# Attention with memory and a feed-forward block: second buffers for the loads of k and v

## The chip, the cores and the metric

One core of a Trainium2 chip. The core has a matrix engine (TensorE, PE; PEld are its weight loads), a vector engine (VectorE, DVE), a scalar engine (ScalarE, ACT), a general engine (GpSimd, POOL) and a queue engine (SyncE, SP), which here issues every transfer between memory and the core's on-chip memory (SBUF). Each engine works through its own instructions in order and waits for the others by semaphores. Matrix products land in accumulator banks (PSUM). The metric is the time of one execution on the device in microseconds (us).

## The reference

The attention is computed for 4 batches and 8 heads of 576 tokens and 64 columns; its output is the input of a feed-forward block over 2304 tokens.

```python
scores = scale * np.matmul(q, k.transpose(0, 1, 3, 2))      # causal mask, softmax -> a
local = np.matmul(a, v)
mem_ret = np.einsum('bhsd,bhde->bhse', q_p, M_prev)          # q_p = phi(q), phi(x) = elu(x) + 1
mem_norm = np.einsum('bhsd,bhd->bhs', q_p, z_prev)[..., None] + 1e-06
x = g * mem_ret / mem_norm + (1 - g) * local                 # g = sigmoid(beta), one per head
h = x @ w_in                                                 # 512 -> 2048
out = np.maximum(h, 0.0) ** 2 @ w_out                        # 2048 -> 512
```

## The kernel before

The work has four kinds of pieces.

*The weights.* w_in and w_out arrive as 64-bit floats in 32 pieces of 512 KB (`load_weight`, L197: tiles raw, xw, hw) and each is split into a high and a low part by DVE and ACT (`split_weight`, L167 to L173, tile w). The pieces come in four stages; the raw tiles of a later stage lie where those of an earlier stage lay, so they can be loaded when these have been split. raw23 is the first piece of the third stage.

*The first tokens.* Tokens 0 to 63 of every head are done at the start in one go (`first_tokens`), in a pool `tp` of their own that is given back afterwards. mask0 is the causal mask of their 64 by 64 scores.

*The attention units.* 24 units, each of a batch, a pair of heads and two or four query tiles (tiles 1 and 2, or 3 and 4, of 128 tokens). `loads` brings a unit's k (kd, L340), its memory and q (qm, L344) and its v (vv, L347). In `attention` PE makes scores (sp, L468), DVE masks and reduces them (L472), ACT takes the exponential (L484); DVE finds the largest entry of v (vx, L400) and makes a scaled copy of v in 16 bits (vs, L417); the probabilities are split (L521, L523), transposed by a transfer (aT, L527) and multiplied with v on PE (acc, L548 to L553), summed on DVE (s, L555), and added by POOL to the memory's share (pm, L435; memx, L560). The result is stored to memory (xd, L572). The first two units use v itself (L542) instead of vs. The next unit's loads are asked for in the middle of a unit. q has two buffers, kd and vv one each.

*The feed-forward blocks.* Nine blocks of 256 tokens (`moe`): tiles of up products (L626 to L628), the square of the positive part on ACT, POOL and DVE, and down products (L616 to L618). Block 0 is the first tokens. The tokens of block 1 are those of units 0 to 3, and `prefetch` loads them back (xn, L592) and transposes them on PE (px, L595).

The order on each engine isn't the order of the code: a scheduler simulates the program at build time with its own costs and issues what it finds ready, by the place in the code as priority. A buffer that is free earlier moves instructions on all engines. On SP the transfers are issued strictly in that order, so one that waits for its buffer holds up all behind it.

Of the kernel before, what the change touches and what calls it, by code (L numbers as in the profile page):

```python
# [8 lines left out]
F32 = mybir.dt.float32  # L9
# [8 lines left out]
B, H, S, D = 4, 8, 576, 64  # L18
# [3 lines left out]
P = 128  # L22
# [21 lines left out]
PXE = 'aa'  # L44
PHI = 1
QB = 2
VVB = 1
ZW = D + 1
MW = 576
WSC = 1.0 / 256.0  # L50
EB = 3
RB = 1
KB = 1
XB = 2
PJ = 6
SEQ = 'a0 b0 g a1 r b1 r c0 l r r c1'
# [34 lines left out]
def fused_kernel(ctx: ExitStack, tc: tile.TileContext, t0_d, zt_d, kk_d, qv_d, beta, w_in, w_out, out):  # L91
    nc = tc.nc
    w_in = w_in.bitcast(U32)
    w_out = w_out.bitcast(U32)
    cp = ctx.enter_context(tc.tile_pool(name="cp", bufs=1))
# [11 lines left out]
    mask = cp.tile([P, MW], BF16, name="mask")  # L107
# [19 lines left out]
    def gates():  # L127
# [9 lines left out]
        for b in range(GB):  # L137
            nc.vector.tensor_copy(gpb[:, b * NP : (b + 1) * NP], gp)
        nc.vector.tensor_scalar(out=g1b, in0=gpb, scalar1=-1.0, scalar2=1.0, op0=ALU.mult, op1=ALU.add)

    mask0 = cp.tile([P, D], F32, name="mask0")
    nc.vector.tensor_copy(mask0[:D], mask[:D, 448 : 448 + D])
    nc.vector.tensor_copy(mask0[D:], mask[D:, 512 : 512 + D])

    wsrc = []
    for j in range(4):
# [52 lines left out]
    def weights():  # L199
        n0 = 0  # L200
        for n, ex in STG:
            n1 = n0 + n + len(ex)
            dpl = ctx.enter_context(tc.tile_pool(name=f"wd{n0}", bufs=1, reuse_waits="tile"))
            plain = range(n0 + len(ex), n1) if XF else range(n0, n0 + n)
            heads = []
            for m in range(n0, n1):
                if m in wt:
                    continue
                two = PAIR and m % 2 == 0 and m in plain and m + 1 in plain and m >= PAIR - 1
                wp[m] = dpl.tile([P, 2, 1024 if two else 512], F32R, name=f"w{m}")  # L210
                heads.append(m)
                for u in range(2 if two else 1):
                    wt[m + u] = wp[m][:, :, u * 512 : (u + 1) * 512]
            with ExitStack() as st:
                tp = st.enter_context(tc.tile_pool(name="tp", bufs=1, reuse_waits="tile")) if n0 == 0 else None
                spl = st.enter_context(tc.tile_pool(name=f"ws{n0}", bufs=1, reuse_waits="tile")) if n else None
                where = list(ex) + [spl] * n if XF else [spl] * n + list(ex)
                if n0 == 0:
                    first_tokens(tp, lambda: load_weight(heads[len(raw)], where[heads[len(raw)]]))
                    yield  # L220
                for m in range(n0, n1):
                    if m in heads:
                        if m not in raw:
                            load_weight(m, where[m - n0])
                        split_weight(m)
                    yield
            n0 = n1

    def first_tokens(tp, ahead):
        me, ze, se, xe, ye = ([nc.gpsimd if c == "p" else nc.vector for c in t] for t in TE)  # L230
        xh = mo.tile([P, NK, BLK], F32R, tag="xh", name="xh", bufs=2)
        xl = mo.tile([P, NK, BLK], F32R, tag="xl", name="xl", bufs=2)
        xq.append((xh, xl))
        ng = B // GB
        bc = [P, GN, D]
        tr, sp, wt0, wx = ({} for _ in range(4))
# [100 lines left out]
    def loads(b, p, tiles):  # L337
        qa, qb = QT[tiles[0]][0], sum(QT[tiles[-1]])
        kd = at.tile([P, S], F32, tag="kd", name="kd", bufs=KB)
        nc.sync.dma_start(kd[:, :qb], kk_d[b, p, :, :qb])  # L340
        qm = at.tile([P, 2 * ZW + SQ], F32, tag="qm", name="qm", bufs=QB)
        qa, qb = qa - D + 2 * ZW, qb - D + 2 * ZW
        for c0, c1 in [(0, qb)] if qa == 2 * ZW else [(0, 2 * ZW), (qa, qb)]:
            nc.sync.dma_start(qm[:, c0:c1], qv_d[b, p, :, c0:c1])  # L344
        vv = at.tile([P, 5 * P], F32, tag="vv", name="vv", bufs=VVB)
        nv = (tiles[-1] + 1) * P
# [431 lines left out]
```

## Time and profile before

| | |
|---|---|
| median of three runs | 617.59 us (617.44 to 619.06) |
| the profiled execution | 617.12 us, of which the span from first to last instruction is 615.0 us |
| PE busy | 567.4 us (92%) |
| DVE busy | 403.6 us (66%) |
| ACT busy | 329.8 us (54%) |
| POOL busy | 186.9 us (30%) |
| mean granted clock of PE | 0.980 of full speed |

An engine's busy time is read against a stretch and not against the whole: the kernel's start is work of DVE and ACT, its end is work of PE alone. The matmuls overlap in the array, so busy time says where PE idles, not how fast it goes; the granted clock says that.

### The profile page before, as it was taken

The page shows a single profiled execution, that of the slowest core. Times are in us where ns is not written, and L with a number is a line of the kernel's source. Part 1 is how long each engine was busy: PE and PEld are TensorE (multiplying, and loading weights), DVE is VectorE, ACT ScalarE, POOL GpSimd, SP SyncE. Part 2 cuts the span into 40 slices and gives each one's busy share as a digit, 9 for nine tenths or more (in the row PEclk, how much of TensorE's full clock was granted, in tenths as well). Part 3 has the DMA queues.
Part 4 walks back from the last instruction along what each step waited for, and adds up shares of the span by engine and source line. Part 5 has one row for each costly group of instructions (what it writes and reads, how often), then busy time and mean ns, then how long its engine had stood idle before and what let it go on. Part 6 is the DMA issues. An engine that isn't in the chain of part 4 may idle for free.

```text
span 615.0 us, 11584 instructions
## 1 busy us (share of the span) xinstructions
PE 567.4 (92%) x4198; PEld 482.9 (79%) x4198; DVE 403.6 (66%) x1247; ACT 329.8 (54%) x748; POOL 186.9 (30%) x179
## 2 busy tenths in 40 slices
PE   2267899599999998999999999999999999999997
PEld 2156797388888886888888888788888899998996
DVE  3999878677779876988788787797887511001000
ACT  1597777465676744666566544665466412322312
POOL 1410305226563651224331323232322121221221
PEclk9996799899999999999999999999999999999999
DMA  5939296577556755577555555665546320200000
GB/s 179 400 145 377 49 269 147 130 139 163 122 116 145 174 100 130 125 162 150 134 114 131 100 129 122 142 181 122 112 89 117 74 48 1 68 1 1 35 0 35
DMA packets 128392, 76.54 MB, mean 124 GB/s; under 512 B 99920, under 2 KB 113232, under 8 KB 128336
## 3 DMA queue, kind: packets, MB, share of 16 engines
q1 hardware_dynamic: 128336, 75.81, 49.9%
q8 instruction: 33, 0.54, 0.4%
q14 instruction: 23, 0.19, 0.1%
HBM read 42.76 MB, written 8.91 MB: 84 GB/s over the span
## 4 chain that ended last, share of the span: by engine, by line
PE 78%; DMA 8%; DVE 8%; issue 2%; POOL 1%; ACT 1%; SPq 1%; DVEq 0%; POOLq 0%; ACTq 0%
PE up L626 11%; PE up L628 11%; PE up L627 11%; PE oacc L616 10%; PE oacc L618 10%; PE oacc L617 10%; PE sp L468 7%; DMA vv<-in_qv_dram 3%; PE acc L553 2%; PE pm L435 2%; DMA aT<-a 2%; DMA raw<-in_w_in_dram 2%; PE acc L550 1%; PE acc L548 1%; PE acc L542 1%
## 5 line engine op out<-in xcount | busy, mean ns | idle before, releaser
L626 PE MATMUL up<-xh,w 128*128 128x256 f32 x576 | 166.9, 290 | 0.7 <-DVE xl L599 0.6
L628 PE MATMUL up<-xh,w 128*128 128x256 f32 x576 | 166.1, 288 | 0.0
L627 PE MATMUL up<-xl,w 128*128 128x256 f32 x576 | 165.6, 288 | 0.0
L641 POOL TENSOR_TENSOR gl<-r,gh 128x512 fp32r<-128x512 f32 x72 | 100.1, 1390 | 207.2 <-DVE gh L640 121.4
L626 PEld LDWEIGHTS up<-xh,w 128*128 128x128 f32 x576 | 110.8, 192 | 8.6 <-issue 4.3
L484 ACT ACTIVATE e<-e,mx 128x320 f32<-128x320 f32 (+3 forms) x128 | 77.9, 611 | 71.8 <-DVE mx L472 70.6
L616 PE MATMUL oacc<-w,gh 128*128 128x512 f32 x288 | 115.4, 401 | 0.4 <-ACT gh L638 0.4
L627 PEld LDWEIGHTS up<-xl,w 128*128 128x128 f32 x576 | 110.8, 192 | 4.8 <-issue 2.0
L628 PEld LDWEIGHTS up<-xh,w 128*128 128x128 f32 x576 | 110.8, 192 | 3.9 <-issue 2.9
L617 PE MATMUL oacc<-w,gh 128*128 128x512 f32 x288 | 113.8, 395 | 0.0
L618 PE MATMUL oacc<-w,gl 128*128 128x512 f32 x288 | 110.2, 397 | 0.3 <-POOL gl L641 0.3
L632 ACT ACTIVATE r<-up 128x512 f32<-128x512 f32 x72 | 42.6, 592 | 112.1 <-PE up L628 104.1
L523 DVE SCALAR_TENSOR_TENSOR a<-e,a 128x128 f16<-128x128 f32 x120 | 78.7, 669 | 25.4 <-ACT a L521 25.1
L634 POOL TENSOR_TENSOR r<-r 128x512 f32<-128x512 f32 x40 | 45.0, 1124 | 136.5 <-ACT r L632 136.5
L640 DVE CAST gh<-r 128x512 fp32r<-128x512 f32 x40 | 16.9, 423 | 93.8 <-ACT r L636 90.6
L616 PEld LDWEIGHTS oacc<-w,gh 128*128 128x128 f32 x288 | 54.3, 189 | 11.5 <-issue 1.5
L618 PEld LDWEIGHTS oacc<-w,gl 128*128 128x128 f32 x288 | 53.0, 188 | 12.6 <-issue 1.4
L617 PEld LDWEIGHTS oacc<-w,gh 128*128 128x128 f32 x288 | 54.3, 189 | 9.2 <-issue 0.7
L472 DVE CUSTOM_DVE_ANT_0 e<-sp,mask 128x320 f32<-128x320 f32 (+3 forms) x128 | 56.6, 474 | 7.3 <-PE sp L468 6.9
L521 ACT ACTIVATE a<-e 128x128 f16<-128x128 f32 x120 | 57.0, 522 | 3.2 <-DMA aT<-a 1.7
L553 PE MATMUL acc<-vs,aT 128*128 128x128 f16 x308 | 37.0, 221 | 0.0
L550 PE MATMUL acc<-vs,aT 128*128 128x64 f16 x308 | 35.7, 193 | 0.0
(130 smaller groups left out, 883.0 us busy)
## 6 DMA issues: line engine op xcount, KB each, us to landing
raw<-in_w_in_dram SPq DMA_DIRECT2D x11, 512.0 KB, 8.7
vv<-in_qv_dram SPq DMA_DIRECT2D x16, 320.0 KB, 2.9
raw<-in_w_out_dram SPq DMA_DIRECT2D x9, 512.0 KB, 7.0
kd<-in_kk_dram SPq DMA_DIRECT2D x16, 288.0 KB, 3.1
xd<-memx SPq DMA_DIRECT2D x32, 128.0 KB, 2.1
xn<-xd SPq DMA_DIRECT2D x16, 256.0 KB, 3.0
out_dram<-o SPq DMA_DIRECT2D x16, 256.0 KB, 2.2
qm<-in_qv_dram SPq DMA_DIRECT2D x8, 321.0 KB, 3.2
```

Of the source, the lines that this page charges most:

```text
L472: nc.vector.tensor_tensor_reduce(out=e[:n, h, ks], in0=sps[:n, h, :w], in1=mask[:n, 448 - q0 + s * w : 448 - q0 + s * w + w], scale=-0.125 ...
L484: nc.scalar.activation(e[:n, h, :ke], e[:n, h, :ke], AF.Exp, bias=bs, scale=-1.0, accum_out=sm[:n, h : h + 1])
L521: nc.scalar.mul(av[:, :, o0 : o0 + w], x, SC)
L523: nc.vector.scalar_tensor_tensor(out=av[:, :, o0 + w : o0 + 2 * w], in0=x, scalar=SC, in1=av[:, :, o0 : o0 + w], op0=ALU.mult, op1=ALU.sub ...
L553: nc.tensor.matmul(o2, aT[:, h * nb + c, :n], vs[:, h, c], start=False, stop=c == i)
L616: nc.tensor.matmul(acc[t], gh[:, u, ts], w_out_op(f, 0), start=f == 0, stop=False)
L617: nc.tensor.matmul(acc[t], gh[:, u, ts], w_out_op(f, 1), start=False, stop=False)
L618: nc.tensor.matmul(acc[t], gl[:, u, ts], w_out_op(f, 0), start=False, stop=f == NF - 1)
L626: nc.tensor.matmul(up[:, u, :], w_in_op(f, k, 0), xh[:, k, :], start=k == 0, stop=False)
L627: nc.tensor.matmul(up[:, u, :], w_in_op(f, k, 0), xl[:, k, :], start=False, stop=False)
L628: nc.tensor.matmul(up[:, u, :], w_in_op(f, k, 1), xh[:, k, :], start=False, stop=k == NK - 1)
L641: nc.gpsimd.tensor_tensor(out=gl, in0=r, in1=gh.bitcast(F32), op=ALU.subtract)
```

## The change

kd and vv get a second buffer each, and mask0 moves from the pool that lives as long as the kernel into the first tokens' pool, made there by the same two copies. Lines after it move up by four and, behind first_tokens, by one.

```diff
-VVB = 1
+VVB = 2
-KB = 1
+KB = 2
...
-    mask0 = cp.tile([P, D], F32, name="mask0")
-    nc.vector.tensor_copy(mask0[:D], mask[:D, 448 : 448 + D])
-    nc.vector.tensor_copy(mask0[D:], mask[D:, 512 : 512 + D])
...
+        mask0 = tp.tile([P, D], F32, name="mask0")
+        nc.vector.tensor_copy(mask0[:D], mask[:D, 448 : 448 + D])
+        nc.vector.tensor_copy(mask0[D:], mask[D:, 512 : 512 + D])
```

The order of the instructions that come out of the scheduler moves at many places. On SP, in the first 20 us, behind the first tokens' last load; kd_327, qm_329 and vv_331 are the loads of unit 1. Before:

```order
L258 DMA tr1_120<-in_t0_dram 128x1024
L344 DMA qm_329<-in_qv_dram 128x386
L197 DMA raw4_363<-in_w_out_dram 128x1024
L197 DMA raw5_379<-in_w_out_dram 128x1024
L197 DMA raw6_408<-in_w_out_dram 128x1024
L197 DMA raw7_415<-in_w_out_dram 128x1024
L197 DMA raw8_430<-in_w_in_dram 128x1024
L197 DMA xw_463<-in_w_in_dram 128x512
L197 DMA xw_464<-in_w_in_dram 128x512
L340 DMA kd_327<-in_kk_dram 128x320
```

and with the change:

```order
L257 DMA tr1_120<-in_t0_dram 128x1024
L339 DMA kd_327<-in_kk_dram 128x320
L343 DMA qm_329<-in_qv_dram 128x386
L346 DMA vv_331<-in_qv_dram 128x384
L193 DMA raw4_363<-in_w_out_dram 128x1024
L193 DMA raw5_379<-in_w_out_dram 128x1024
L193 DMA raw6_408<-in_w_out_dram 128x1024
L193 DMA raw7_415<-in_w_out_dram 128x1024
```

kd_327 and vv_331 have moved ahead of the weights raw4 to raw8; vv_331 stood 23 rows further down, as the first row of the next piece.

On SP again, from there to the third stage's first weights, raw23; the numbers 776, 774 and 778 belong to unit 3, 481 to unit 2 and 870 and 872 to unit 4. Before:

```order
L347 DMA vv_331<-in_qv_dram 128x384
L344 DMA qm_776<-in_qv_dram 128x386
L572 DMA xd0_92<-memx_314 128x2x128
L340 DMA kd_774<-in_kk_dram 128x320
L347 DMA vv_481<-in_qv_dram 128x384
L527 DMA_TRANSPOSE aT_791<-a_790 128x10x128
L197 DMA raw23_663<-in_w_out_dram 128x1024
L197 DMA raw24_670<-in_w_in_dram 128x1024
```

and with the change:

```order
L343 DMA qm_776<-in_qv_dram 128x386
L571 DMA xd0_89<-memx_314 128x2x128
L339 DMA kd_870<-in_kk_dram 128x576
L346 DMA vv_778<-in_qv_dram 128x384
L526 DMA_TRANSPOSE aT_791<-a_790 128x10x128
L571 DMA xd0_89<-memx_448 128x2x128
L526 DMA_TRANSPOSE aT_791<-a_790 128x6x128
L343 DMA qm_872<-in_qv_dram 128x130
L343 DMA qm_872<-in_qv_dram 128x256
L193 DMA raw23_663<-in_w_out_dram 128x1024
L193 DMA raw24_670<-in_w_in_dram 128x1024
```

The loads of k and v are now those of one unit later, and unit 4's q (qm_872), which stood behind the third stage's weights, stands ahead of raw23.

On DVE, around unit 3's two last sums (s3_907 and s3_935), with unit 4's scores (e_1394) beside them. Before:

```order
L417 SCALAR_TENSOR_TENSOR vs_858<-vv_778,vy_848,vs_858 128x3x64 x2
L532 RECIPROCAL sm_879<-sm_879 128x2
L532 RECIPROCAL sm_913<-sm_913 128x2
L400 TENSOR_REDUCE vx_1326<-vv_875 128x1
L472 ISA e_1394,mx_1395<-sp_1397,mask_76 128x288
L472 ISA mx_1395 128x1
L402 TENSOR_SCALAR vx_1326<-vx_1326 128x1
L555 TENSOR_REDUCE s3_907<-acc_896 128x128
L555 TENSOR_REDUCE s3_935<-acc_928 128x128
```

and with the change:

```order
L471 ISA e_1394,mx_1395<-sp_1397,mask_76 128x288
L471 ISA mx_1395 128x1
L165 SCALAR_TENSOR_TENSOR xw_734<-xw_734 128x256
L163 TENSOR_SCALAR hw_726<-hw_726 128x512
L554 TENSOR_REDUCE s3_907<-acc_896 128x128
L554 TENSOR_REDUCE s3_935<-acc_928 128x128
L169 TENSOR_TENSOR w29_716<-hw_719,w29_716 128x512
L399 TENSOR_REDUCE vx_1446<-vv_1354 128x1
L389 SCALAR_TENSOR_TENSOR pe_1442<-qm_1351,pe_1442 128x256
L169 TENSOR_TENSOR w31_718<-xw_733,w31_718 128x256
L165 SCALAR_TENSOR_TENSOR hw_726<-hw_726 128x512
```

The reduction of the next unit's v no longer stands in front of the sums, and the last weight splits (L169, before L173) have moved behind them.

## Rows read from the trace of the kernel before

**Rows 1.** Windows: stretch, length, busy PE, PEld, DVE, ACT, POOL, clock, DMA, GB/s

```profile
0.00:46.10 46.10, 17.54 (x178) 12.92 (x178) 35.12 (x94) 25.97 (x57) 12.80 (x17) 1.00 0.65 241
57.70:124.20 66.50, 57.73 (x351) 46.81 (x349) 51.54 (x156) 45.38 (x105) 17.86 (x18) 0.91 0.61 164
124.20:230.00 105.80, 105.14 (x817) 88.51 (x816) 83.93 (x260) 67.26 (x164) 53.77 (x63) 0.99 0.64 136
230.00:247.00 17.00, 14.64 (x119) 12.11 (x118) 12.23 (x36) 8.40 (x19) 3.54 (x4) 1.00 0.55 134
247.00:615.00 368.00, 363.89 (x2709) 316.20 (x2707) 210.31 (x672) 174.25 (x382) 98.09 (x77) 1.00 0.41 91
...
15.40:30.80 15.40, 3.34 (x19) 1.75 (x16) 15.09 (x37) 9.05 (x18) 7.68 (x7) 1.00 1.03 400
```

**Rows 2.** Timeline of PE: start, length, instruction [idle before, what ended it]

```profile
63.21 2.52 PE L542 MATMUL acc<-vv,aF 64*128 64x64 f32 x12 [1.88 <-DMA vv<-in_qv_dram]
...
83.52 0.67 PE L435 MATMUL pm<-qm,pe 128*128 128x130 f32 x4
...
122.40 1.87 PE L468 MATMUL sp<-kd,qm 64*128 64x448 f32 x4 [4.96 <-DMA kd<-in_kk_dram]
124.20 1.26 PE L595 MATMUL px<-identr,xn 128*128 128x128 f32 x8
```

**Rows 3.** Windows behind those two idle times, columns as in rows 1

```profile
64.00:72.00 8.00, 8.00 (x40) 7.15 (x38) 8.00 (x20) 7.17 (x21) 2.83 (x2) 0.57 0.00 0
119.00:126.00 7.00, 3.60 (x23) 2.34 (x24) 3.48 (x13) 3.08 (x8) 0.00 (x0) 0.51 0.75 212
```

**Rows 4.** Timeline of SP's queue: issue, length, transfer

```profile
61.38 0.34 SPq L340 DMA_DIRECT2D kd<-in_kk_dram  x1
73.17 0.33 SPq L347 DMA_DIRECT2D vv<-in_qv_dram  x1
...
75.56 0.49 SPq L197 DMA_DIRECT2D raw<-in_w_out_dram  x1
...
84.22 0.81 SPq L344 DMA_DIRECT2D qm<-in_qv_dram  x2
...
118.21 0.38 SPq L572 DMA_DIRECT2D xd<-memx  x1
...
120.08 0.80 SPq L592 DMA_DIRECT2D xn<-xd  x2
```

**Rows 5.** Timeline of DVE: its waits on v and on the third stage's weights

```profile
76.51 0.55 DVE L400 TENSOR_REDUCE vx<-vv 128x1 f32<-128x384 f32 x1 [1.93 <-DMA vv<-in_qv_dram]
...
79.56 0.43 DVE L167 TENSOR_SCALAR raw<-raw 128x512 uint32<-128x512 uint32 x1 [1.07 <-DMA raw<-in_w_out_dram]
...
81.54 0.43 DVE L167 TENSOR_SCALAR raw<-raw 128x512 uint32<-128x512 uint32 x1 [1.50 <-DMA raw<-in_w_in_dram]
...
114.37 0.82 DVE L400 TENSOR_REDUCE vx<-vv 128x1 f32<-128x640 f32 x1 [2.94 <-DMA vv<-in_qv_dram]
...
115.92 0.75 DVE L555 TENSOR_REDUCE s<-acc 128x128 f32<-128x256 f32 x2
...
235.59 0.82 DVE L400 TENSOR_REDUCE vx<-vv 128x1 f32<-128x640 f32 x1 [2.76 <-DMA vv<-in_qv_dram]
```

**Rows 6.** Groups by line on DVE: shapes, count | busy us, mean ns | idle before

```profile
L405 DVE TENSOR_REDUCE vy<-vt 128x1 f32<-128x128 f32 x22 | 6.2, 281 | 1.9 <-PE vt L404 1.9
L169 DVE SCALAR_TENSOR_TENSOR hw<-hw 128x512 uint32<-128x512 uint32 x8 | 6.0, 745 | 0.0
L173 DVE TENSOR_TENSOR w<-hw,w 128x512 fp32r<-128x512 f32 x8 | 5.4, 680 | 0.0
L173 DVE TENSOR_TENSOR w<-xw,w 128x256 fp32r<-128x256 f32 x8 | 3.5, 442 | 1.2 <-ACT w L172 1.2
L402 DVE TENSOR_SCALAR vx<-vx 128x1 uint32<-128x1 uint32 x22 | 3.2, 145 | 0.1
L142 DVE CAST mask<-mask 64x64 f32<-64x64 bf16 x1 | 0.2, 186 | 0.0
```

## The prediction

> **What bounds the kernel now.** I read first the busy time of each engine by stretch, then the idle times of the matrix engine (TensorE, PE) in its timeline with what ended each, and last the queue of the loads (SP) and the vector engine (DVE) around those places.
>
> By stretch [rows 1]: up to 46.1 us PE works 17.5 us and DVE 35.1: the weights are split and the first tokens computed, and DVE is the limit (15.09 of 15.40 us between 15.4 and 30.8). From 57.7 to 124.2 PE works 57.73 of 66.50 us, 8.77 idle, at a mean clock of 0.91. After that it idles 0.66 of 105.8 us, 2.36 of the 17 us from 230 to 247, and 4.11 of the last 368, most of it the drain at the end. So from about 124 us on the kernel is as long as its matmuls; a change of buffers can win only what stands idle or runs slowly before 124 us, and the 2.4 us at 230 to 247.
>
> PE's idle times in the first place have names [rows 2]: 1.88 us until unit 1's v lands (63.21), and 4.96 us until a load of k lands (122.40), with the transposes of the next MoE block's tokens (px, 124.20) behind it. After each of the two the granted clock falls to 0.5, the lower level of 1.2 GHz [rows 3]: first between 64 and 72 us (the mean over 64 to 72 is 0.57, so (1 - 0.57) x 8 = 3.4 us of full-rate work is lost), and again from 119 (0.51 over 119 to 126).
>
> The cause is one step back, in SP's queue [rows 4]. With one buffer the load of unit 2's v waits for the last product with unit 1's v: SP stands from 61.38+0.34 to 73.17 and nothing behind it leaves, the first weights of the third stage (raw, 75.56) among them. DVE feels each such load [rows 5]: its reduction of v (vx) waits 1.93 us at 76.51, 2.94 at 114.37 and 2.76 at 235.59.
>
> **The change part by part.** *Where the mask lies.* The two casts (the first 186 ns, the second alike [rows 6]) stay at their place as the vector engine's second and third row and are read only by the first tokens' softmax: cost nothing. They free 256 bytes a partition for good, against 2304 + 2560 taken by the second kd and vv. No instruction is added; all the rest is order.
>
> *Unit 1's k and v* (160 + 192 KB) now stand before the four loads of w_out (raw4 to raw7), v having stood 23 rows further down the queue. So the 1.88 us wait on v goes. If the clock then stays up, 3.4 us more go: PE would be up to 5.3 us earlier by about 71 us. This is no gain of the total yet; what PE does next must be ready. What it may cost is the four weight loads behind: 352 KB at the 400 GB/s of 15.4 to 30.8 us is 0.9 us each. I take nothing, since DVE, which splits them, is busy 15.09 of 15.40 us there with work already landed; if that cover is gone, 0.9.
>
> The Trainium skill speaks against this part: "DMA: Bandwidth & Descriptors", section "Issuing engines are not separate DMA queues", says that all loads share the same 16 engines and interleave, so an earlier load is paid for by another. The trace agrees that they are full there (share 1.03); by that rule alone the sum would be 0.9 us worse, by the row of DVE unchanged.
>
> *The third stage's weights move the wrong way.* Before, raw23 left at 75.56, ahead of unit 4's q (qm, 84.22). Now both pieces of unit 4's q stand ahead of it, and their buffer is unit 2's, free only when PE has done unit 2's memory product (pm, 83.52 to 84.19 before [rows 2]). PE has about the same work ahead of pm as before (96 up and 16 down products where 84 and 24 stood), so pm comes 1.88 + 3.4 us earlier, ends at 78.9, two issues take 0.81, and raw23 leaves at 79.7. Landing took 4.0 us before (75.56 to 79.56, where DVE waited for it). So DVE starts this split at 83.7 instead of 79.56: +4.1 us. Bounds: +0, if pm were ready early enough for raw23 to leave at 75.56 as before; +9.4, if pm ends at 84.19 as before, so that raw23 leaves at 85.0 and lands at 89.0. I take the value between them that follows from the two gains before it.
>
> *From there to the end of unit 3.* DVE needs 37.1 us from that split (79.56) to the end of unit 3's last sum (s, 115.92 + 0.75). The order now puts five of its rows behind that sum: two L173 on hw, two on xw, one L169 on hw, 2 x 0.68 + 2 x 0.44 + 0.75 = 3.0 us [rows 6]. Seven short ones (L400 0.55, L405 0.28, five of about 0.15 like L402) stand ahead of the split instead, 1.6 us that fall into the wait for the weights. And the wait of 2.94 us on v goes, since that load no longer needs unit 3's buffer. Left: 37.1 - 3.0 - 1.6 - 2.9 = 29.6 us, so the sum ends at 83.7 + 29.6 = 113.3 instead of 116.7.
>
> *From there to the next MoE block.* The chain of sum, POOL, store xd (118.21), load xn (120.08) and px (124.20) took 7.5 us and isn't changed; the product before px that waited for k (1.87 us) falls beside xn's landing and is left out. So px comes at 120.8: 3.4 us earlier. Behind px stands the same matrix work in both orders, 491 us up to the end.
>
> *The later gap.* The 2.36 us at 230 to 247 hang on the v wait of 2.76 at 235.59 and on a transpose; with a free buffer the first goes. But the order of the whole program is dealt anew, and 0.66 us of small waits may come elsewhere. Between 0 and 3.0 gained I take half of the gap, 1.2.
>
> Sum: 617.12 (the profiled execution, span 615.0 and 2.1 around it) - 3.4 - 1.2 = 612.5. The median of the runs shown is 617.59, 0.47 higher, so 613.0.
>
> **Rivals.**
>
> *More is won.* If the weights are no later than DVE needs them, the sum ends at 79.56 + 29.6 = 109.2 and px comes at 116.7: -7.5; with the whole later gap and the small waits, -3.0. 617.59 - 10.5 = 607.1. For it: DVE still waited 1.50 us at 81.54 for the next of these weights, and 1.93 on v before, so it has slack to catch up. Against it: one queue, and q ahead of the weights. PE's own work sets an end: 66.5 - 8.8 idle - 4.9 of half clock (3.4, and 1.5 of the 3.6 us worked between 119 and 126 [rows 3]) leaves 52.8 us from 57.7, px at 110.5, no more than 14 us won.
>
> *Nothing is left.* The waits go, but the newly dealt order has others of the same size: the old one has 3 us in the 350 us after 124, and 4.6 more would eat the forecast: 617.6. For it: in-order queues, and transposing transfers on the same SP queue. Against it: kd and vv loads were among what blocked that queue, and now find a free buffer.
>
> *Slower.* The third stage's weights wait behind unit 4's q, and PE doesn't reach pm early. It decides at 82 us: px is as late as before when the sum ends at 116.7, so the split starts at 87.1, raw23 leaves at 83.1 and pm ends at 82.3. If pm ends at 84.2 as before, raw23 leaves at 85.0, the split starts at 89.0 and the sum ends at 118.6: px 1.9 us later than before. PE then idles in one piece for the third stage's products, and the clock falls once more, 3.4 us. With nothing won later: 617.59 + 5.3 = 622.9. For it: PE's order before pm now holds 48 up products in a row, and the scalar engine, which has to empty their banks, has copies and weight splits queued between. Against it: the 1.88 us wait is certainly gone.
>
> *The change doesn't do what it says*, the loads not moving: excluded by the order itself, where kd and vv of the next unit stand up to 23 rows earlier.
>
> **How the numbers follow.** About 0.3% (1.9 us) is what a measurement of this kernel tells from no change. Forecast, 609 to 615.7: 0.48. More is won, below 609: 0.22. Nothing left, 615.7 to 619.5: 0.15. Slower: 0.15. So faster 0.70, same 0.15, slower 0.15. For 8 in 10 the range goes from 605.5 (towards the 14 us that PE's work allows) to 619.0, leaving most of the slower case out; the forecast's own range is 609 to 615.7.
>
> **What would show it.** Right: no wait of PE on vv near 62 us and no clock of 0.50 between 64 and 71; unit 2's pm near 78 us and raw23's issue right behind unit 4's two q pieces; DVE waiting some 3 us for raw23; hardly any wait of vx on vv; px near 121 us; after px as much PE time as before. Wrong: px at or after 124 us, with raw23 leaving after 83; or PE idle over 5 us after px; or px before 117, in which case the weights were not the limit.

## The result, and the profile after

The changed kernel takes 621.31 us (median of 14 runs) where the kernel before takes 617.58 (14 runs beside them): a ratio of 1.0065, 95% interval 1.0042 to 1.0088. One of its 14 runs, of 1840.56 us, was slow and is left out of the ratio; the other 13 have the median 621.01. It is slower; 613.0 was forecast.

The start went as forecast, or better. In the timeline of PE there is no wait for v near 62 us any more (1.88 us before [rows 2]), unit 2's pm is at 77.3, and px is at 117.35 us instead of 124.20 (120.8 forecast). Ahead of px PE waits for DVE, and behind it come waits that the kernel before has not, or shorter. Timeline of PE, changed kernel (start, length, instruction, idle time before it and what ended it):

```profile
77.34 0.67 PE L434 MATMUL pm<-qm,pe 128*128 128x130 f32 x4
...
106.38 0.22 PE L547 MATMUL acc<-vs,aT 128*128 128x128 f16 x1 [1.82 <-DVE vs L416]
108.73 1.33 PE L467 MATMUL sp<-kd,qm 64*128 64x288 f32 x4 [1.45 <-DVE mx L471]
...
117.35 0.53 PE L594 MATMUL px<-identr,xn 128*128 128x128 f32 x4
118.79 0.53 PE L594 MATMUL px<-identr,xn 128*128 128x128 f32 x4 [0.91 <-DMA xn<-xd]
...
235.83 0.40 PE L467 MATMUL sp<-kh,qh 64*128 64x288 f32 x2 [1.06 <-DVE mx L471]
...
238.97 0.29 PE L547 MATMUL acc<-vs,aT 128*128 128x128 f16 x1 [2.05 <-DMA aT<-a]
...
253.61 0.46 PE L594 MATMUL px<-identr,xn 128*128 128x128 f32 x4
...
259.78 0.22 PE L403 MATMUL vt<-identb,vx 128*128 128x128 bf16 x1
...
385.92 0.22 PE L552 MATMUL acc<-vs,aT 128*128 128x128 f16 x1
...
393.60 0.53 PE L594 MATMUL px<-identr,xn 128*128 128x128 f32 x4 [2.12 <-DMA xn<-xd]
396.56 0.75 PE L594 MATMUL px<-identr,xn 128*128 128x128 f32 x4 [2.42 <-DMA xn<-xd]
```

The stretches answer to rows 1 and 3 (length, busy PE, PEld, DVE, ACT, POOL, clock, DMA share, GB/s):

```profile
57.70:124.20 66.50, 60.14 (x377) 48.31 (x377) 60.74 (x175) 50.70 (x116) 20.84 (x19) 0.93 0.64 174
124.20:230.00 105.80, 105.80 (x818) 88.93 (x817) 80.58 (x256) 67.03 (x161) 52.38 (x62) 1.00 0.63 137
230.00:247.00 17.00, 13.90 (x86) 11.91 (x86) 10.01 (x30) 6.21 (x14) 3.50 (x3) 0.80 0.52 120
...
64.00:72.00 8.00, 8.00 (x56) 6.80 (x55) 8.00 (x19) 8.00 (x21) 2.98 (x2) 1.00 0.10 31
108.00:114.00 6.00, 5.21 (x14) 3.21 (x15) 6.00 (x13) 4.20 (x9) 4.38 (x6) 0.51 1.03 224
...
234.00:246.00 12.00, 8.90 (x60) 7.71 (x59) 7.25 (x24) 5.63 (x12) 3.50 (x3) 0.72 0.59 119
390.00:406.00 16.00, 11.26 (x92) 9.64 (x91) 9.67 (x31) 7.22 (x20) 0.00 (x0) 0.79 0.59 123
```

From 64 to 72 us the clock is now 1.00 (0.57 before). From 230 to 247 it is 0.80 and PE does 86 products where it did 119 at a clock of 1.00; from 390 to 406 it is 0.79. The same two windows of the kernel before:

```profile
234.00:246.00 12.00, 9.64 (x79) 8.12 (x77) 8.72 (x25) 4.46 (x11) 2.66 (x3) 1.00 0.41 92
...
390.00:406.00 16.00, 15.65 (x119) 13.11 (x116) 12.97 (x49) 9.33 (x24) 4.02 (x3) 1.00 0.58 121
```

Idle time alone doesn't show the loss: PE idles 46.4 us of the span after (621.9 - 575.5 busy) and 47.6 before. A product at half clock counts as busy. So I estimate the work: each product by its distance from start to start at full clock in the timeline (an up product 0.12 us, a down product 0.23, scores 0.095 to 0.155 by width, a product with v 0.03 or 0.06). *Lost* is the length of a stretch less the work that was started in it, and takes idle time and half clock together; like the work, it is an estimate. It is summed for the profiles of both kernels and for the experiments that the account rests on (us):

| kernel | 0-90 | 90-140 | 140-230 | 230-250 | 250-380 | 380-410 | 410-600 | sum |
|---|---|---|---|---|---|---|---|---|
| before | 46.0 | 13.7 | 5.8 | 3.3 | 4.7 | 2.1 | 2.1 | 77.7 |
| same order as before (e5) | 44.1 | 13.9 | 6.1 | 6.0 | 4.7 | 2.1 | 2.2 | 79.0 |
| changed | 41.3 | 16.5 | 5.0 | 6.7 | 5.1 | 8.4 | 3.1 | 86.0 |
| changed, again (e3) | 42.1 | 15.3 | 5.2 | 5.8 | 5.3 | 9.2 | 2.9 | 85.7 |
| px later at block 4 (e4) | 41.4 | 16.1 | 5.0 | 5.6 | 4.9 | 3.3 | 3.8 | 80.0 |
| vx of unit 14 later (e6) | 42.2 | 15.2 | 4.6 | 0.3 | 5.3 | 2.7 | 2.4 | 72.6 |
| e6 again (e15) | 42.3 | 16.1 | 5.0 | 0.8 | 4.9 | 2.4 | 2.7 | 74.2 |
| both (e8) | 42.3 | 16.5 | 5.2 | 0.5 | 5.8 | 1.3 | 2.0 | 73.5 |
| before, vx later (e13) | 47.4 | 14.8 | 5.7 | 1.1 | 6.3 | 5.8 | 3.6 | 84.7 |
| before, both (e14) | 45.1 | 14.4 | 6.0 | 0.7 | 6.4 | 1.3 | 2.7 | 76.7 |

One profile is one execution: rows with the same order differ by some 3 us in a stretch (3.3 and 6.0 from 230 to 250 us; 44.1 and 47.4 up to 90 us, where e13 still has the order of the kernel before). Both profiles of the changed kernel (623.7 and 624.5 us) are among its longest executions (617.97 to 624.45 in e3), so the table shows its loss larger than the medians do; why the profiled ones fall there, no run here shows.

### The profile page after: what moved, and what is told of

The parts are those of the page before. It is cut to its first block, busy times and chain, and to the rows that moved or that the text cites. A ratio compares the mean times of both kernels' runs of the same rounds, so it can differ in the third digit from the quotient of the medians.

```text
span 621.9 us, 11587 instructions
## 1 busy us (share of the span) xinstructions
PE 575.5 (93%) x4198; PEld 488.6 (79%) x4198; DVE 401.7 (65%) x1247; ACT 331.9 (53%) x748; POOL 188.0 (30%) x179
## 4 chain that ended last, share of the span: by engine, by line
PE 70%; DVE 13%; DMA 8%; ACT 4%; issue 3%; POOL 1%; SPq 1%; DVEq 0%; POOLq 0%; ACTq 0%
PE up L625 10%; PE up L627 10%; PE up L626 10%; PE oacc L615 9%; PE oacc L616 8%; PE oacc L617 8%; PE sp L467 7%; DMA raw<-in_w_in_dram 3%; DVE w L169 2%; PE acc L552 2%; DMA vv<-in_qv_dram 2%; PE pm L434 2%; DVE e L471 2%; PE acc L541 1%; PE acc L549 1%
## 5 line engine op out<-in xcount | busy, mean ns | idle before, releaser
L554 DVE TENSOR_REDUCE s<-acc 128x128 f32<-128x256 f32 x60 | 24.3, 418 | 23.6 <-PE acc L552 21.8
```

## The experiments

All times are medians; the ratio is against runs of the kernel before on the same chip in the same call, with its 95% interval.

**The changed kernel again (e3).** No edit.

> The changed kernel once more, unaltered, for a second profile beside the others of this chip. My theory: the two gaps of the first profile (230 to 250 us and 385 to 410 us) are there again at the same places with the half clock behind them, 3.4 and 6 us more lost there than in the kernel before, and about 2.6 us won up to 126 us; total 619 to 624. Rival (the gaps of one execution are chance): the idle pieces stand at other places and the total is within 1 us of the kernel before.

621.18 us, ratio 1.0044 (1.0019 to 1.0069). The waits are there again at the same places: px 2.25 us at 393.27 and 2.66 at 396.68, 1.07 at 236.25 and 2.02 at 239.36. The gaps belong to the order.

**The mask alone (e5).** `VVB = 1`, `KB = 1`, the mask as in the change.

> Only the first tokens' mask moves to the first tokens' own pool; k and v keep one buffer. The order on the matrix engine and on the load queue is word for word that of the kernel before. Both theories: the same time as before, within 1 us. A difference would mean that the place of the mask in memory matters.

618.32 us, 1.0014 (0.9992 to 1.0037): no difference. The mask's place costs nothing.

**Each buffer alone (e1, e2).**

```diff
-VVB = 2      (e1: k alone)
+VVB = 1
...
-KB = 2       (e2: v alone)
+KB = 1
```

> Second buffer for k alone (v has one, the mask lies in the first tokens' pool). My theory: the two buffers win a few us before the first px and the order that is dealt anew behind it decides the rest, so the total need not be the sum of parts. With one buffer for v the wait of the matrix engine on v near 62 us and the drop of the clock behind it come back (about 1.9 us idle near 62 us and 3.4 us of half clock), and the total lies between 612 and 624. What tells: idle pieces of 1 us and more behind 124 us with the clock at 0.5 after them make up the difference to 617.6. Rival (the loss comes with k's second buffer, whose load gets ahead of the tokens' load xn in the queue): 620 to 624 with px waiting over 2 us for xn. Rival (the loss comes with v's second buffer): 613 to 618.

> Second buffer for v alone (k has one, the mask lies in the first tokens' pool). My theory: no wait on v near 62 us, a clock of 1.00 from 62 to 72 us, so some 5 us won by 72 us as in the changed kernel; behind that another order with gaps of its own, total between 610 and 622. Rival (k's second buffer makes the loss, since its load gets ahead of xn): 612 to 615, and px waits under 1 us for xn everywhere. Rival (v's second buffer makes the loss): 620 to 624.

e1: 625.36 us, 1.0106 (1.0069 to 1.0143). e2: 624.15 us, 1.0088 (1.0054 to 1.0121). By its median each part alone is slower than both together (621.18 in the same call), though the intervals touch or overlap; so the parts don't add, and each has an order of its own. Both times lie above the range that was expected, and details of both expectations failed. e1 has no wait for v near 62 us but one of 2.26 us for POOL at 70.75; it loses 10.5 us from 60 to 90, where the changed kernel loses 2.4. e2 wins the early 5 us and loses 12.9 from 140 to 230, with px waiting 2.96 us for xn at 191.76, where k's second buffer, which the rival blames, isn't there. So k's second buffer can't be the only cause, nor v's.

**px later behind one block (e4).** The order up to about 384 us is that of the changed kernel.

```diff
-            if j == PJ and n + 1 < NBLK:
+            if j == (7 if n == 4 else PJ) and n + 1 < NBLK:
```

> The changed kernel, with the tokens of one MoE block (the one after block 4) transposed one pair of up products later. Up to about 384 us the matrix engine's order is word for word that of the changed kernel. My theory (px stands too near behind the sum whose store it needs, the clock falls behind the wait): the two waits of px for xn (2.1 and 2.4 us) go, and the half clock behind them, so 5 to 6.5 us are won: about 615.5, range 614 to 617.5, and the clock stays at 1.00 from 390 to 405 us. Rival (the time is lost all along, to loads sharing the engines and the memory; the gap only shows it): under 1.5 us won, 620 to 621.5. Rival (a gap taken away comes back at the next px): px at 455 us waits instead, 619 to 621.

618.53 us, 0.9998 (0.9978 to 1.0019): 2.65 us less than e3 on the same chip. In its profile the gap is gone as expected and the clock stays up; first its timeline of PE, then its window.

```profile
392.88 0.54 PE L594 MATMUL px<-identr,xn 128*128 128x128 f32 x4 [0.23 <-DMA xn<-xd]
394.19 0.50 PE L594 MATMUL px<-identr,xn 128*128 128x128 f32 x4 [0.77 <-DMA xn<-xd]
```

```profile
390.00:406.00 16.00, 15.00 (x122) 12.16 (x121) 12.74 (x44) 8.92 (x23) 2.87 (x3) 1.00 0.78 201
```

The profiles differ by 6.8 us (624.45 and 617.67) and the medians by 2.65, half of what I expected: the mechanism holds, its size in an average run is smaller.

Why px waited: from the last product of the sum that it needs (385.92 + 0.22 = 386.1) PE reached px at 391.5 (393.60 - 2.12), after 5.3 us of other work. The tokens took 7.5 us to come: sum, store, load, landing. The kernel before has 7.5 us of work there, and px doesn't wait; its timeline of PE, from the last product of the sum to px:

```profile
381.15 0.22 PE L553 MATMUL acc<-vs,aT 128*128 128x128 f16 x1
...
388.85 0.37 PE L595 MATMUL px<-identr,xn 128*128 128x128 f32 x3
```

Counted in the same way from the built order of each kernel, the work between that sum and px puts the waits for xn at this block nearly in order: 4.9 us (changed) waits 2.1 and 2.4; 5.1 (e11) 2.71; 5.7 (e13) 2.45; 6.8 (e1) 1.50; 6.9 (e6) 1.06; 7.2 (before) none; 7.3 (e4) 0.23 and 0.77; 7.3 (e10) 0.17; 8.6 and more (e8, e9, e12, e14) none.

The second half of px waited once more, since xn landed late: 3.1 and 5.7 us from issue to landing, 2.6 and 2.9 before. SP's queue, changed kernel:

```profile
388.18 0.66 SPq L571 DMA_DIRECT2D xd<-memx  x1
389.73 0.33 SPq L339 DMA_DIRECT2D kd<-in_kk_dram  x1
390.45 0.80 SPq L591 DMA_DIRECT2D xn<-xd  x2
```

A load of k (288 KB) has gone out just ahead of xn; in the kernel before it follows xn (385.72, 386.90). "DMA: Bandwidth & Descriptors" of the Trainium skill, section "Issuing engines are not separate DMA queues", says that all transfers share the same 16 engines and interleave; these landings agree. In e4 k also goes ahead, and xn lands after 3.4 and 4.2 us, so k's load is at most a part of it; it was not tried alone.

**vx of one unit later (e6, again as e15).** DVE's timeline shows what starts the gap at 235 us: DVE stands 4.12 us for the v of unit 14, whose product vt is at 259.78, 28 us later. The rows that transposes and scores wait for stand behind it.

```profile
231.75 0.82 DVE L399 TENSOR_REDUCE vx<-vv 128x1 f32<-128x640 f32 x1 [4.12 <-DMA vv<-in_qv_dram]
```

In SP's queue this load leaves behind unit 14's q and xn:

```profile
223.66 1.67 SPq L343 DMA_DIRECT2D qm<-in_qv_dram  x2
226.65 0.80 SPq L591 DMA_DIRECT2D xn<-xd  x2
227.56 0.36 SPq L346 DMA_DIRECT2D vv<-in_qv_dram  x1
```

In the kernel before vx is for unit 13 at this place, waits 2.76 [rows 5], and its vt is at 244.25, 8.7 us later: with one buffer the load must wait until the v before has been used, so the reduction can't run far ahead. The gap itself isn't new: behind its wait the kernel before has waits of PE of 0.94 and 1.42 us (its lines stand in the last section). Nor has the sum of vx's waits on v changed much; first the kernel before, then the changed one (us, times):

```profile
  DMA vv<-in_qv_dram: 17.0, 14
```

```profile
  DMA vv<-in_qv_dram: 15.5, 11
```

The edit lets unit 14's vx take its tile from another ring, so that it stands some 20 rows further back; PE's order ahead of this place is unchanged.

```diff
-            vx = at.tile([P, 1], F32, tag="vx", name="vx", bufs=2)
+            vx = at.tile([P, 2], F32, tag="vz", name="vx", bufs=2)[:, :1] if (b, p, tiles) == order[14] \
+                else at.tile([P, 1], F32, tag="vx", name="vx", bufs=2)
```

> The changed kernel; only the tile that unit 14's reduction of v (vx) writes is taken from another ring, so that the reduction stands some 20 rows later on the vector engine and behind its load by more time. Up to the products near 230 us the matrix engine's order is word for word that of the changed kernel. My theory (the second buffer lets the load and the reduction move ahead together, so the vector engine still waits for a v that is needed only units later, 4.1 us at 231.75): the waits of the matrix engine at 235.8 and 239.0 us (3.1 us) and the half clock behind them go, 3 to 5 us. The order behind is dealt anew; the matrix work that stands between the last sum of the block and px is 6.9 us there instead of 4.9, so the wait of px at 393 us shrinks too. Total 613 to 618. Rival (the transposes or the memory are late at 235 us whatever the vector engine does): the waits at 236 and 239 us stay, and the total is 617 to 622.

611.66 us, 0.9897 (0.9876 to 0.9918), 6 us under the kernel before; 613 to 618 was too careful. Its windows show a clock of 1.00 and no idle time in either stretch (px, at 384.20 here, waits 1.06 us), and DVE meets a v that is there:

```profile
234.00:246.00 12.00, 12.00 (x107) 10.14 (x106) 11.53 (x33) 7.04 (x15) 4.69 (x4) 1.00 0.58 136
390.00:406.00 16.00, 16.00 (x136) 13.46 (x134) 11.85 (x42) 11.07 (x22) 5.23 (x5) 1.00 0.53 135
```

```profile
238.12 0.81 DVE L399 TENSOR_REDUCE vx<-vv 128x1 f32<-128x640 f32 x1
```

The transposes and the memory were not late. The later gap shrank with it, since this order has 6.9 us of work ahead of px there.

**Both gaps (e8), and px later behind every block (e7).** e8 is e4's and e6's edits together; e7 is `PJ = 7`.

> The changed kernel with unit 14's reduction of v later (as in the run before this) and the tokens of the block after block 4 transposed one pair of up products later: 8.9 us of matrix work between the last sum and that px. My theory: both late gaps are gone, of the 9.5 us that they cost more than before in the first profile some 8 are back, and what was won up to 126 us (2.6 us) is left: 612.5 to 616, so faster than the kernel before by 2 to 5 us. Rival (what was won early is lost anyway, in waits that are named nowhere): 617.5 to 620.

> The changed kernel with the tokens of every next MoE block transposed one pair of up products later. The order is dealt anew from the first block on: 8.0 us of matrix work stand between the last sum and the first px instead of 3.5, and 13.8 instead of 4.9 at the block near 390 us. My theory: no wait of px over 0.5 us near 390 us and none near 118 us, clock up behind both; a gap of the vector engine's wait on v may come anywhere. Total 612 to 619. Rival (the waits move, the total stays): 619.5 to 623.

e8: 611.16 us, 0.9899 (0.9871 to 0.9927), under the 612.5 to 616 that was expected and not to be told from e6. e7: 617.29 us, 0.9985 (0.9964 to 1.0005): px waits nowhere over 0.2 us, but vx waits 3.15 us at 207.69 and 3.48 at 231.28, and PE behind them.

**The reduction held back everywhere (e9, e10), with px later too (e12).** e9: `bufs=1` for vx. e10: e6's edit for units 9 and on. e12: e10 and px later behind blocks 0 and 4.

> The changed kernel with one buffer instead of two for the result of the reduction of v (vx), so that no unit's reduction can stand ahead of the use of the one before; two buffers each for k and v stay. The order is dealt anew from about 75 us on. My theory (the second buffer of v costs where the reduction is pulled ahead with the load, and the vector engine waits in order for a v that is not needed yet): the vector engine waits under 6 us in all on v (15.5 in the changed kernel), no wait of the matrix engine over 1 us behind 130 us that hangs on such a wait, 15 us of matrix work between the last sum and px near 390 us. Total 609 to 615. Rival (the win of the run with unit 14 alone was a lucky order): anywhere from 616 to 622.

> As the run with unit 14's reduction of v later, but for all units from unit 9 on; the order up to about 170 us is that of the changed kernel. 7.3 us of matrix work between the last sum and px near 390 us. My theory: the waits of the vector engine on v behind 190 us (11 us in the changed kernel) go for the greater part, and the two late gaps with them: 609.5 to 614. Rival (only the gap at 235 us was on the path, and another deal is as good or bad as any): 614 to 622.

> The reductions of v later from unit 9 on, and the next block's tokens transposed one pair of up products later behind blocks 0 and 4 (8.0 and 9.2 us of matrix work between the last sum and px). My theory: as the run with both gaps taken away, and about 1 us more from the wait of px near 118 us: 609 to 613. Rival (near 118 us the vector and scalar engines set the pace, so a later px wins nothing): 611 to 615.

e9: 614.65 us, 0.9949 (0.9925 to 0.9973). vx waits for no load (15.5 us in the changed kernel), as its summary of the line shows, with no row under "sat idle". From 234 to 246 and from 390 to 406 us PE is busy all the time at a clock of 1.00; but the first px waits 3.06 us, and 17.0 us are lost from 90 to 140 and 7.7 from 140 to 230.

```profile
L399 DVE TENSOR_REDUCE vx<-vv x22: 535/806/810, 68.9 to 439.0; 128x1 f32<-128x640 f32 x16, 128x1 f32<-128x384 f32 x6
its engine sat idle before it (us, times) until:
```

e10: 612.65 us, 0.9913 (0.9882 to 0.9944). e12: 610.63 us, 0.9878 (0.9843 to 0.9914), the fastest median here; its interval overlaps those of e6, e8 and e10. The first px no longer waits in e12, but 15.3 us are still lost from 90 to 140, so near 118 us px alone isn't the limit.

**k's second buffer once more (e11).** e9 with `KB = 1`.

> Two buffers for v, one for k, and one for the result of the reduction of v. Beside the run with two for k it tells what k's second buffer is worth once the early reductions are gone. 5.1 us of matrix work stand between the last sum and px near 390 us (as in the changed kernel, 4.9). My theory: px near 390 us waits over 3 us again and the clock falls behind it, 5 to 7 us; the gap near 235 us is gone; total 614 to 619. Rival (the waits on k's load alone decide): 609 to 613, or over 620 with waits on kd.

616.92 us, 0.9989 (0.9964 to 1.0013), 2.3 us more than e9 with intervals that overlap; the time is as expected, with the wait of px that was read from the order:

```profile
389.26 1.19 PE L594 MATMUL px<-identr,xn 128*128 128x128 f32 x8 [2.71 <-DMA xn<-xd]
```

**What the second buffers are worth (e13, e14 against e15).** The kernel before, with unit 13's vx from another ring (e13), and with px later behind block 4 as well (e14).

```diff
-            vx = at.tile([P, 1], F32, tag="vx", name="vx", bufs=2)
+            vx = at.tile([P, 2, D], F32, tag="s3", name="vx", bufs=2)[:, 0, :1] if (b, p, tiles) == order[13] \
+                else at.tile([P, 1], F32, tag="vx", name="vx", bufs=2)
```

> The kernel before (one buffer each for k and v), with unit 13's reduction of v written to a tile of another ring, so that it stands some 17 rows later on the vector engine; up to about 230 us the order is that of the kernel before. It asks what the second buffers are worth once the wait near 236 us is gone. My theory: the waits of the matrix engine at 240 and 243 us (2.4 us) and what is lost beside them go, 3 us; but only 5.7 us of matrix work stand between the last sum and px near 390 us instead of 7.2, so px waits there, 2 to 5 us with the clock: 615 to 620. Rival (the wait alone decides): 612.5 to 614.5.

> As the run before this, and the next block's tokens transposed one pair of up products later behind block 4: 8.6 us of matrix work between the last sum and px near 390 us. Theory one (the second buffers are worth the 1 to 3 us that the ledger shows won up to 230 us): 613 to 615.5, slower than the changed kernel with the two gaps taken away (611.2) by 2 to 4 us. Theory two (the second buffers are worth nothing, all was the order): 610 to 612.5.

> The changed kernel with unit 14's reduction of v later, unaltered from its first run, beside the two runs of the kernel before without its wait, on the same chip. Expected as in the first run: 609.5 to 613, and 0.8 to 1.2 per cent under the kernel before.

e13: 622.66 us, 1.0077 (1.0056 to 1.0098), above my 615 to 620. The gap at 240 us is gone (1.1 lost), and px waits instead, as the order said; 1.4 us more than in the kernel before are lost up to 90 us, where the order is the same; the other profiles of this order lose 44.1 to 46.0 there, and what makes the difference no run shows.

```profile
395.05 0.75 PE L595 MATMUL px<-identr,xn 128*128 128x128 f32 x4 [2.45 <-DMA xn<-xd]
```

e14: 614.87 us, 0.9953 (0.9935 to 0.9972). e15: 612.71 us, 0.9897 (0.9868 to 0.9926). The intervals don't overlap. With the late waits taken away on both sides the second buffers win 2.2 us by the medians, 3.5 by the ratios (0.0056 x 618.3). The table has as much up to 230 us, where the early waits are: 63.4 lost in e15, 65.5 in e14. It is one order on each side, so another pair of orders may give another figure.

## Why the prediction was wrong

*Unit 1's k and v.* Right: no wait on v, clock of 1.00 from 64 to 72 us. Nothing shows of a cost in the four weight loads behind them: DVE is busy 15.29 of 15.40 us from 15.4 us on (15.09 before [rows 1]).

*The third stage's weights.* Right within a microsecond: pm ends at 78.0 (78.9 forecast), raw23 leaves at 78.91 (79.7), and DVE starts the split at 83.00 (83.7) after 3.60 us of waiting.

```profile
78.04 0.82 SPq L343 DMA_DIRECT2D qm<-in_qv_dram  x2
78.91 0.42 SPq L193 DMA_DIRECT2D raw<-in_w_out_dram  x1
```

```profile
83.00 0.43 DVE L163 TENSOR_SCALAR raw<-raw 128x512 uint32<-128x512 uint32 x1 [3.60 <-DMA raw<-in_w_out_dram]
...
109.50 0.74 DVE L554 TENSOR_REDUCE s<-acc 128x128 f32<-128x256 f32 x2
```

*From there to the end of unit 3, and to px.* Right, a little careful: 27.2 us (83.00 to 110.24) where 29.6 was forecast, then 7.1 (7.5). px came 6.85 us earlier, not 3.4; with e3 and e5 for the second profile of each order (118.02 and 121.87) it is 3.9 to 6.9.

*"Behind px stands the same matrix work in both orders, 491 us up to the end."* This is the step that failed. From px to the end it took 504.6 us (621.9 - 117.35). The work is the same; the time that is lost beside it is not, and I gave the new order that of the old one. By the table, the changed kernel (mean of its two profiles) against the order before (mean of two):

- up to 90 us 3.4 us are won (41.7 against 45.1);
- from 90 to 140 us 2.1 are given back: PE comes earlier to work that DVE hands out (DVE is busy 60.74 us of 66.5 up to 124.2, 51.54 before [rows 1]), waits 1.82 and 1.45 us for it at 106.38 and 108.73, and the clock falls from 108 to 114. That DVE is the limit is argued; no run took work off it there;
- from 230 to 250 us 1.6 more are lost, less than the two profiles of the order before differ there, so this part isn't shown;
- from 380 to 410 us 6.7 more, the one large part. In e4, which takes this gap away, the medians give back 2.65.

The transposes of the blocks tell where the lead went without an estimate, since ahead of the first and of the third px the same products stand in both orders. The first px leads by 6.85 us. The third px stands at 253.61 us (253.04 in e3), and in the kernel before at the same time (254.35 in e5):

```profile
253.69 0.46 PE L595 MATMUL px<-identr,xn 128*128 128x128 f32 x4
```

So what the start had won was gone before the gap at 390 us made the kernel slower, and without that gap (e4) it takes the time of the kernel before.

Two of the prediction's signs spoke: vx still waits 15.5 us on v, where hardly any wait was to be seen, and PE idles 10.0 us behind px (3.6 before), where over 5 was named as wrong.

*"The later gap."* Wrong: none of the 1.2 us came. I took half of the gap at 230 to 247 as won, because v would find a free buffer. It did, and the scheduler used the freedom to move the load and the reduction behind it a unit ahead together. The reduction still stands close behind its load, in an engine that works in order; it now waits 4.12 us instead of 2.76, for a value needed 28 us later. PE's waits there sum to 3.11 us instead of 2.36. Holding that one reduction back (e6), with the order that is dealt behind it, turns the changed kernel from 0.4 to 0.7% slower into 1.0% faster.

*The rivals.* "Nothing is left" had the right kind of cause, new waits from a newly dealt order, but summed idle times only; the half clock behind two of them made them worth more than they were long. "Slower" gave a near price (622.9) for a reason that didn't come: pm was early. That it is near is luck.

*What stays open.* Why the profiled executions of the changed kernel are among its longest, and with that how much of the 6.7 us at 380 to 410 an average run loses (e4 says 2.65). What part k's load ahead of xn has in xn's late landing. Between the first and the third px, where the lead goes, only some waits have names, and no run shows what would keep it.

## What to carry to other kernels

A second buffer is not only a wait less: where a scheduler deals the order, the load and its first reader move ahead together, and an early reader on an in-order engine can block work that is due now (here one of 22 such readers was shown to, e6). Look for waits on values that are needed much later, and hold such readers back. Before trusting a gain at the start, count in the new order how much work stands between each producer and the consumer that must wait for it through memory; against a latency of about 7.5 us here, px with 5 to 6 us of work ahead of it waited 2.5 to 4.5 us, with about 7 up to 1.5, and with 8.6 or more not at all.

## What the runs showed of the hardware

Two waits of 2.1 and 2.4 us close together cost more than they are long: 8.4 us are lost from 380 to 410 where the kernel before loses 2.1, with a clock of 0.79 over 390 to 406 us.

Whether the clock falls behind waits of about 1 us differs from one execution of the same order to the next. The kernel before has two at 240 us and keeps 1.00 over 234 to 246:

```profile
240.35 0.40 PE L468 MATMUL sp<-kh,qh 64*128 64x288 f32 x2 [0.94 <-DVE mx L472]
...
243.45 0.23 PE L548 MATMUL acc<-vs,aT 128*128 128x128 f16 x1 [1.42 <-DMA aT<-a]
```

e5 has the same order on PE and the same two waits, and its clock is 0.72 over 236 to 248:

```profile
238.24 0.40 PE L467 MATMUL sp<-kh,qh 64*128 64x288 f32 x2 [0.94 <-DVE mx L471]
...
241.36 0.29 PE L547 MATMUL acc<-vs,aT 128*128 128x128 f16 x1 [1.43 <-DMA aT<-a]
```

```profile
236.00:248.00 12.00, 9.63 (x60) 7.68 (x60) 9.30 (x28) 6.51 (x15) 2.31 (x2) 0.72 0.52 100
```

So the 0.72 that the changed kernel has at this place, behind waits of 1.06 and 2.05 us, can't be put down to its longer waits.

The runs of the kernel before spread from 615.5 to 620.9 us in one call and from 613.2 to 623.2 in another. Those of the changed kernel go with the mean granted clock only in part: 618.7 us at 0.977 and 623.4 at 0.969, but 621.6 at 0.985.
